# Attention and two feed-forward layers on one core: softmax sums from a column of ones, more engine choices, a new order

## The chip, the core and the metric

The kernel runs on one core of a Trainium2 chip. A core has TensorE (matmul), VectorE, ScalarE, GpSimd and a queue, SyncE, from which the DMAs are issued here. The metric is the device time of one execution in microseconds; the median of three runs of the kernel before is 1056.15 us (1055.23 to 1056.76).

## What is computed

```python
scores = (1/sqrt(D)) * q @ k.T + bias      # B=4, H=8, S=576, D=64; bias from a small MLP over positions
scores = scores - max(scores); attn = exp(scores)
attn = attn / (sum(attn) + 1e-09)
x = attn @ v                               # to 2304 tokens x 512
h = x @ w_in;  g = s * relu(h)**2 + b;  x = g @ w_out        # layer 1, 512 -> 2048 -> 512
h = x @ w_in2; g = h - tanh(h);         out = g @ w_out2     # layer 2, 512 -> 2048 -> 512
```

The weights come in 64-bit floats and are converted on the chip; matrices are split into an upper and a lower 16-bit part, and a product is three matmuls.

## The kernel before

The program is a list of tasks that a planner puts in order when the kernel is built. `Schedule.add` takes a task with the engines that may run it and the planner's cost on each, its predecessors, a priority (a due time) and the buffers that it takes or uses. `forward` then walks through a modelled time and picks, among the tasks that can start first, the one of lowest priority. Tables at the top of the file steer it: `COST` and `XFER` scale the costs of operations and transfers, `ENGINE` and `ONLY` narrow a task or a kind of task to certain engines, `SHIFT` moves the priority of each task (names such as `u13.hi`: unit group 13, step `hi`). The order on each engine's queue in the chip is fixed by this plan.

Attention has 144 units of 128 rows by 576 keys, in 36 groups of four (`unit_tasks`, `unit_rest`). One unit runs: score matmuls (`qk`, line 1041, two buffers `sp`); bias added and row maximum taken on VectorE (`ttr`, 1073); the maximum is shifted by a constant (`mx_add`, 1081, VectorE or GpSimd); the exponential on ScalarE (`ex`, 1087), which also accumulates the row sum into a column of `sum`; the upper 16-bit part (`hi`, 1097 on VectorE, 1099 on ScalarE); the lower part in two pieces (`lo_a`, `lo_b`, 1104, VectorE or GpSimd); a transposing DMA (`tr`, 1119); and the product with the values (`pv`, 1132 and 1138), nine and five matmuls of 64 columns into `xp`. There is one `xp` buffer for a group of four units. `x_tasks` then turns a group into tokens: epsilon on the sums (1176), reciprocal (1180), scaling of `xp` to `xf` (1188), which frees `xp`, upper and lower part, squares, and a transposing DMA.

`moe1_tasks` is layer 1, in nine blocks of 256 tokens: `ph` matmuls (1573), rectifier on ScalarE (1586), square (1591), upper and lower part (1597, 1599, 1603), `po` matmuls (1645), evacuation (1659, 1664). Layer 1 runs between the units of attention and goes on behind them. When attention has ended its buffers are given up (`turn`), and the weights of layer 2 are loaded, converted (1253, 1256, 1259), and split into seven combinations for each half (`w2_split`: upper part 615, sums 1852, lower part 618). Layer 2 (`in_product`, line 2038, and `out_product`, line 2166) is 18 half blocks of seven products each way. An `in_product` is evacuated to SBUF on ScalarE (`copy`, 2057) or VectorE (2064), goes through `tanh` (2074) and a subtraction (2083), and is combined with others (2092) and split for the next product. Before, `ONLY` keeps the subtractions, additions and sums of this part on VectorE.

Of the kernel before, what the change touches and what calls it, by code (L numbers as in the profile page):

```python
# [2326 lines left out]
```

## Time and profile before

| | |
|---|---|
| median of three runs | 1056.15 us |
| the profiled execution | 1057.96 us |
| its span, first to last instruction | 1056.2 us |
| TensorE matmul busy | 964.1 us (91%) |
| VectorE busy | 881.6 us (83%) |
| ScalarE busy | 667.5 us (63%) |
| GpSimd busy | 250.1 us (24%) |
| mean granted TensorE clock | 0.954 |

Busy shares are means over parts of the run with different limits. The rows further down give them by stretch, then who waits for whom, then the cost of single operations. In them PE is TensorE, PEld its weight load, DVE VectorE, ACT ScalarE, POOL GpSimd; a granted clock of 1.00 is the 2.4 GHz level, 0.50 the 1.2 GHz level.

### The profile page before, as it was taken

The page shows a single profiled execution, that of the slowest core. Times are in us where ns is not written, and L with a number is a line of the kernel's source. Part 1 is how long each engine was busy: PE and PEld are TensorE (multiplying, and loading weights), DVE is VectorE, ACT ScalarE, POOL GpSimd, SP SyncE. Part 2 cuts the span into 40 slices and gives each one's busy share as a digit, 9 for nine tenths or more (in the row PEclk, how much of TensorE's full clock was granted, in tenths as well). Part 3 has the DMA queues.
Part 4 walks back from the last instruction along what each step waited for, and adds up shares of the span by engine and source line. Part 5 has one row for each costly group of instructions (what it writes and reads, how often), then busy time and mean ns, then how long its engine had stood idle before and what let it go on. Part 6 is the DMA issues. An engine that isn't in the chain of part 4 may idle for free.

```text
span 1056.2 us, 32450 instructions
## 1 busy us (share of the span) xinstructions
PE 964.1 (91%) x13486; PEld 833.2 (79%) x13486; DVE 881.6 (83%) x1918; ACT 667.5 (63%) x1307; POOL 250.1 (24%) x319
## 2 busy tenths in 40 slices
PE   5676678999988999999997999988999999999998
PEld 3233356778767788788886888878999999999998
DVE  6999899876568677786774889999999999999885
ACT  4797659749767565776853687766554555464452
POOL 6146437247542334455511000000000000000000
PEclk9767679899999999999999999998999999999999
DMA  9969995899999879999896904410001100100000
GB/s 341 398 227 216 311 236 119 184 200 252 245 197 230 168 179 176 201 188 207 171 180 104 397 21 138 148 36 12 32 23 32 52 23 22 42 22 23 22 22 22
DMA packets 261444, 153.66 MB, mean 145 GB/s; under 512 B 197680, under 2 KB 229552, under 8 KB 261296
## 3 DMA queue, kind: packets, MB, share of 16 engines
q1 hardware_dynamic: 261296, 151.59, 59.1%
q8 instruction: 105, 1.72, 0.7%
q14 instruction: 43, 0.35, 0.1%
HBM read 84.03 MB, written 20.33 MB: 99 GB/s over the span
## 4 chain that ended last, share of the span: by engine, by line
PE 43%; DVE 9%; ACT 3%; DMA 2%; issue 2%; POOL 1%; SPq 0%; DVEq 0%; ACTq 0%; POOLq 0%
PE acc L2166 14%; PE pa L2038 9%; PE pb L2038 7%; PE po L1645 5%; PE ph L1573 4%; PE po L2166 2%; DMA et<-hl 2%; DVE w2big L1852 2%; DVE w2big L618 1%; PE sp L1041 1%; DVE w1big L618 1%; ACT e L1087 1%; POOL hl L1104 1%; PE xp L1132 1%; DVE hr L1603 1%
## 5 line engine op out<-in xcount | busy, mean ns | idle before, releaser
L1645 PE MATMUL po<-hr,w1big 128*128 128x256 f16 x1728 | 202.9, 274 | 3.6 <-ACT x L1664 2.7
L1104 POOL TENSOR_TENSOR hl<-e,hl 128x64 f16<-128x64 f32 (+1 forms) x200 | 160.2, 818 | 184.9 <-ACT hl L1099 107.2
L1573 PEld LDWEIGHTS <-w1big 128*128 128x128 f16 x1728 | 166.9, 99 | 31.5 <-issue 10.6
L1645 PEld LDWEIGHTS <-w1big 128*128 128x128 f16 x1728 | 165.5, 98 | 26.5 <-issue 7.1
L2038 PEld LDWEIGHTS <-w2big 128*128 128x128 f16 x3024 | 175.2, 99 | 2.2 <-issue 2.1
L2166 PEld LDWEIGHTS <-w1big 128*128 128x128 f16 x3024 | 172.8, 98 | 0.0
L1087 ACT ACTIVATE e<-sp,mx 128x576 f32<-128x576 f32 x144 | 105.6, 735 | 70.3 <-POOL mx L1081 34.3
L1073 DVE CUSTOM_DVE_ANT_0 sp<-sp,bi 128x576 f32<-128x576 f32 x144 | 107.0, 772 | 20.2 <-PE sp L1041 16.2
L1573 PE MATMUL ph<-xt_own,w1big 128*128 128x256 f16 x960 | 113.1, 274 | 3.0 <-ACT r L1586 2.2
L1041 PE MATMUL sp<-ks,qs 64*128 64x288 f16 (+1 forms) x960 | 84.2, 296 | 25.8 <-ACT e L1087 24.8
L1573 PE MATMUL ph<-w1big 128*128 128x256 f16 x768 | 91.2, 276 | 3.3 <-ACT r L1586 2.6
L1041 PEld LDWEIGHTS <-qs 64*128 64x128 f16 (+1 forms) x960 | 48.7, 99 | 53.0 <-issue 42.2
L1132 PEld LDWEIGHTS <-et 128*128 128x128 f16 (+1 forms) x1440 | 54.7, 104 | 41.2 <-issue 21.5
L1132 PE MATMUL xp<-vp,et 128*128 128x64 f16 (+1 forms) x1440 | 65.4, 199 | 19.1 <-DMA et<-hl 11.7
L2166 PE MATMUL acc<-hr,w1big 128*128 128x128 f16 x1296 | 79.9, 219 | 0.0
L1099 ACT ACTIVATE hl<-e 128x576 f16<-128x576 f32 x96 | 64.7, 678 | 23.1 <-DMA et<-hl 20.2
L2166 PE MATMUL acc<-w2big,w1big 128*128 128x128 f16 x1296 | 79.0, 219 | 0.0
L1104 DVE TENSOR_TENSOR hl<-e,hl 128x512 f16<-128x512 f32 (+1 forms) x88 | 48.8, 572 | 15.9 <-ACT hl L1099 13.0
L2038 PE MATMUL pa<-w1big,w2big 128*128 128x128 f16 x960 | 59.9, 219 | 1.7 <-ACT w2big L2057 0.9
L1586 ACT ACTIVATE r<-ph 128x512 f32<-128x512 f32 x72 | 42.3, 590 | 25.8 <-PE ph L1573 21.3
L1591 ACT ACTIVATE r<-r,sq 128x512 f32<-128x512 f32 x72 | 51.2, 718 | 0.9
L2074 ACT ACTIVATE w1big<-w1big 128x512 f32<-128x512 f32 x34 | 21.3, 630 | 45.6 <-DVE w1big L2064 33.4
(229 smaller groups left out, 1757.7 us busy)
## 6 DMA issues: line engine op xcount, KB each, us to landing
bi<-btd SPq DMA_DIRECT2D x64, 288.0 KB, 4.1
w1big<-in_wout SPq DMA_DIRECT2D x12, 1024.0 KB, 6.0
btd<-et SPq DMA_DIRECT2D x36, 295.5 KB, 3.7
w1big<-in_win SPq DMA_DIRECT2D x8, 1024.0 KB, 9.7
w2big<-in_win SPq DMA_DIRECT2D x8, 1024.0 KB, 13.1
x2d<-x SPq DMA_DIRECT2D x36, 128.0 KB, 3.1
w1big<-x2d SPq DMA_DIRECT2D x36, 128.0 KB, 2.3
outT<-xt_own SPq DMA_DIRECT2D x18, 256.0 KB, 2.2
```

The costliest lines, as they stand in the source:

```text
L1041: nc.tensor.matmul(out=out, lhsT=qs.tile[64 * h:64 * h + 64, sq, p * r:p * r + r], rhs=ks.tile[64 * h:64 * h + 64, sk, half * HS:(half + 1 ...
L1073: nc.vector.tensor_tensor_reduce(out=st, in0=st, in1=bi.tile.rearrange("p (a b) -> p a b", a=2), scale=-1.0 / KAP, scalar=3.0e38, op0=ALU. ...
L1087: nc.scalar.activation(out=put(e, row_tile("e")).rearrange("p (a b) -> p a b", a=2), in_=sp.tile[:, :, 0:HS], func=AF.Exp, scale=-1.0, bia ...
L1099: nc.scalar.activation(out=h[:, 0:S], in_=e.tile, func=AF.Copy)
L1104: eng_of(eng).tensor_tensor(out=hl.tile[:, o:o + m], in0=e.tile[:, c:c + m], in1=hl.tile[:, c:c + m], op=ALU.subtract)
L1132: nc.tensor.matmul(out=xp[r0:r0 + r, o:o + 64], lhsT=et.tile[:, n, r0:r0 + r], rhs=vp.tile[:, 0, n % 5, 64 * h:64 * h + 64], start=n == 0, ...
L1573: nc.tensor.matmul(out=ph.tile[:, fi, :], lhsT=win_ap(1, sw, m, f), rhs=xa(sx, m), start=m == 0 and j == 0, stop=m == KM - 1 and j == 2,)
L1586: nc.scalar.activation(out=r.tile, in_=ph.tile, func=AF.Relu)
L1591: nc.scalar.activation(out=r.tile, in_=r.tile, func=AF.Square, scale=sq[:, fp // 4:fp // 4 + 1])
L1645: nc.tensor.matmul(out=po.tile[:, :NB1], lhsT=wout_ap(1, sw, f, c), rhs=rhl[f // 8][:, f % 8, sr, :], start=f == 0 and j == 0, stop=f == K ...
L2038: nc.tensor.matmul(out=bank.tile[:, f * HT:(f + 1) * HT], lhsT=w[:, sw, m, f * 128:(f + 1) * 128], rhs=xs[:, sx, m], start=p in (1, 2, 5) ...
L2166: nc.tensor.matmul(out=bank.tile[:, o + c * HT:o + (c + 1) * HT], lhsT=w[:, sw, f, c * 128:(c + 1) * 128], rhs=g[:, sx, f], start=new and ...
```

## The change

The row sums no longer come from the exponential. The upper part of the values gets a 65th column of ones for each head, so that the product's 65th column is the row sum, and epsilon and reciprocal move behind the product. The shift of the maximum may run on ScalarE, the rectifier of layer 1 on VectorE; the upper halves of layer 2's weights on VectorE or GpSimd as well as ScalarE; the copies of layer 2 on VectorE too, the upper halves of its activations on GpSimd too. The sums of layer 2's weights lose GpSimd. `ONLY` is emptied, and `ENGINE` has 187 entries for 124, among them `"I5.lambda": "pool"`, `"I9.fn": "pool"` and the like for layer 2, and `f0.relu` to `f8.relu` but `f3.relu` on `act`. All entries of `SHIFT` are new, some constants of the planner move.

```diff
-    "u.ex@act": 0.848, "u.hi@act": 0.904, "bias.lambda@act": 1.1, "f.relu@act": 0.952, "f.square@act": 1.15,
+    "u.ex@act": 0.848, "u.hi@act": 1.1413, "bias.lambda@act": 1.1, "f.relu@act": 0.952, "f.square@act": 1.15,
...
-    "scan.fn": (0.80982, 2.01), "u.fn": (1.21869, 1.21), "u.tr": (1.0197, 2.23), "v.fn": (0.97218, 2.27),
+    "scan.fn": (0.80982, 1.99), "u.fn": (1.21869, 0.83), "u.tr": (1.0197, 2.23), "v.fn": (0.97218, 2.25),
...
+    "u12.lo_a": "pool", "u12.lo_b": "pool", "u13.lo_a": "pool", "u13.lo_b": "pool", "u17.lo_b": "pool",
+    "u7.lo_b": "dve", "f7.lo": "dve", "u4.lo_b": "dve", "u18.lo_b": "dve", "u5.hi": "dve", "u4.mx_add": "act",
+    "u7.hi": "act", "u17.lo_a": "pool", "f6.lo": "dve", "f8.hi": "dve", "u13.mx_add": "pool", "u1.lo_a": "pool",
+    "u6.mx_add": "pool", "f5.lo": "pool", "x18.hi": "act", "x13.lo": "pool", "bias2.lambda": "act", "v2.hi":
+    "act", "I5.lambda": "pool", "I0.lambda": "act+pool", "f2.lo": "dve", "u9.lo_b": "pool", "f5.hi": "act",
+    "u1.hi": "act", "u3.mx_add": "pool", "u1.lo_b": "pool", "x14.hi": "dve", "x0.lo": "dve", "x1.lo": "dve",
+    "u4.lo_a": "dve", "x17.lo": "pool", "I0.fn": "pool", "I0.sub": "dve", "I1.lambda": "dve", "I1.sub": "dve",
+    "I4.lambda": "act+dve", "I7.lambda": "act+pool", "X0.xsum": "dve", "bias1.lambda": "act+dve",
+    "bias3.lambda": "act+dve", "f0.relu": "act", "f1.relu": "act", "f2.relu": "act", "f4.relu": "act",
+    "f5.relu": "act", "f6.relu": "act", "f8.relu": "act", "u16.mx_add": "dve+pool", "u17.mx_add": "dve+pool",
+    "u18.mx_add": "act+pool", "s0.lambda": "dve+pool", "I9.lambda": "pool", "P10.lambda": "act+pool", "f1.out":
+    "dve", "u14.mx_add": "dve+pool", "bias4.out": "act", "u16.hi": "act", "u9.hi": "dve", "I9.fn": "pool",
+    "I11.add": "pool", "X2.xsum": "pool", "I17.lambda": "act+dve", "u18.lo_a": "pool", "I3.lambda": "act+pool",
+    "u14.lo_a": "pool", "I14.add": "pool", "I2.fn": "pool", "I15.lambda": "act+dve", "I11.fn": "dve", "I10.fn":
+    "dve", "u8.lo_a": "pool", "x6.lo": "pool", "s2.lambda": "dve+pool", "s6.lambda": "act+pool", "I12.add":
+    "dve", "J11.c22": "dve", "x7.lo": "dve", "x9.lo": "pool", "I8.sub": "pool", "k2.hi": "act", "I1.add":
+    "pool", "s4.lambda": "dve+pool", "I11.lambda": "act+dve", "f0.out": "dve", "f4.out": "dve", "I12.sub":
+    "dve", "u3.lo_a": "dve", "I2.lambda": "act", "X1.lambda": "dve", "I8.add": "dve", "s5.lambda": "act",
+    "bias1.out": "act", "I2.sub": "dve", "f6.hi": "act", "u7.lo_a": "dve", "I13.sub": "dve", "f7.relu": "act",
+    "P00.lambda": "act+pool", "x4.hi": "act", "I6.add": "pool", "X7.lambda": "act", "X1.xsum": "dve", "f8.out":
+    "act", "J5.c22": "dve", "x3.lo": "pool", "I16.lambda": "dve+pool", "f7.out": "act", "I0.add": "dve",
+    "x2.lo": "pool", "I7.add": "pool", "u8.hi": "act", "x5.hi": "act", "x7.hi": "act", "I14.fn": "pool",
+    "u9.lo_a": "dve", "u4.hi": "act", "I5.sub": "pool", "v0.ones": "dve", "f2.out": "act", "J9.fn": "pool",
+    "s7.lambda": "act+pool", "X4.lambda": "act", "I17.fn": "pool", "I10.sub": "dve", "I15.fn": "dve", "x1.hi":
+    "act", "X5.xsum": "dve", "u15.lo_a": "pool", "I13.fn": "pool", "X8.lambda": "act", "J13.fn": "pool",
+    "I16.sub": "pool", "I5.add": "dve", "I5.fn": "dve", "I13.add": "dve", "I10.add": "dve", "I17.add": "dve",
+    "P01.lambda": "act+dve", "J1.fn": "dve", "X6.lambda": "dve", "X5.lambda": "act", "J5.fn": "dve",
+    "I12.lambda": "pool", "I14.lambda": "act+pool", "I4.sub": "pool", "u2.hi": "act", "J3.fn": "dve", "J7.fn":
+    "pool", "x14.lo": "dve", "k3.hi": "dve", "J3.c22": "pool", "X7.xsum": "dve", "u5.mx_add": "act+pool",
+    "I9.add": "pool", "J13.c22": "pool", "I6.fn": "dve", "x17.hi": "dve", "X4.xsum": "dve", "x12.hi": "dve",
+    "x0.hi": "dve", "X3.lambda": "act", "u3.hi": "act", "I11.sub": "pool", "J15.c22": "pool", "I15.sub": "dve",
...
-ONLY = {"I.fn": "dve", "I.sub": "dve", "J.fn": "dve", "J.c22": "dve", "I.add": "dve", "X.xsum": "dve", "P.wsum": "dve"}
+ONLY = {}
...
-    xp_all = ps_x.tile([128, 256], F32, name="xp")
+    xp_all = ps_x.tile([128, 260], F32, name="xp")
...
+            t = vp_p.tile([128, 2 * VW + 10], F16, tag="vp", name="vp")
+            put(vp, (
+                t[:, :VW + 10].rearrange("p (n h d) -> p n h d", h=2, d=65),
+                t[:, VW + 10:].rearrange("p (n h d) -> p n h d", h=2, d=64),
+            ))
...
+        def ones(eng):
+            eng_of(eng).memset(vp.tile[0][:, :, :, 64:65], 1.0)
+        to = sc.add({POOL: 0.2, DVE: 0.1}, ones, [th], due - 2, [], [vp])
...
+            if eng == ACT:
+                nc.scalar.activation(out=m, in_=m, func=AF.Copy, bias=LN_E)
...
-        t_mx = sc.add({DVE: 0.16, POOL: 0.3}, mx_add, [t_ttr[u]], d + 1.5)
+        t_mx = sc.add({DVE: 0.16, POOL: 0.3, ACT: 0.2}, mx_add, [t_ttr[u]], d + 1.5)
...
-                scale=-1.0, bias=mx["m"][:, 0:1], accum_out=sm_i.tile[:, col:col + 1],
+                scale=-1.0, bias=mx["m"][:, 0:1],
...
-                        out=xp[r0:r0 + r, o:o + 64], lhsT=et.tile[:, n, r0:r0 + r],
-                        rhs=vp.tile[:, 0, n % 5, 64 * h:64 * h + 64], start=n == 0, stop=False,
+                        out=xp[r0:r0 + r, o:o + 65], lhsT=et.tile[:, n, r0:r0 + r],
+                        rhs=vp.tile[0][:, n % 5, h], start=n == 0, stop=False,
...
-        te = sc.add({DVE: 0.16, POOL: 0.3}, eps, [t_exp[u] for u in us], d - 3, [], [sum_of[n]])
+            nc.vector.tensor_scalar(
+                out=t, in0=x65()[:, :, 64], scalar1=1e-9 * 2.0 ** 15, scalar2=None, op0=ALU.add
+            )
+        te = sc.add({DVE: 0.18}, eps, [t_pv[u] for u in us], d - 502, [sums], [xp_of[n]], share=0.0)
...
-            tr = sc.add({ACT: 0.21 + 0.8e-3 * 2 * w}, relu, tp + [t_bs], ready - 400, [r], [ph])
+            tr = sc.add(
+                {ACT: 0.21 + 0.8e-3 * 2 * w, DVE: 0.12 + 1.05e-3 * 2 * w}, relu, tp + [t_bs], ready - 400, [r], [ph],
+                share=0.0,
+            )
...
-                {ACT: 1.14}, lambda e: copy_scale(dst(0), src(), w2s["c", g], e), deps + [t_w2c[g]], prio + o
+                {ACT: 1.14, DVE: 0.72, POOL: 3.0}, lambda e: copy_scale(dst(0), src(), w2s["c", g], e), deps + [t_w2c[g]], prio + o
...
-            return [sc.add({POOL: 2.5, DVE: 1.21}, wsum, deps, prio + o)]
+            return [sc.add({DVE: 1.21}, wsum, deps, prio + o)]
...
-                {ACT: 0.68}, lambda _: nc.scalar.activation(out=home(i), in_=bank.tile, func=AF.Copy, scale=ich),
-                [t] + (first_use["E"] if k < 2 else []), pr - 300, [i], [bank],
+                {ACT: 0.68, DVE: 0.66}, lambda e: copy_scale(home(i), bank.tile, ich, e),
+                [t] + (first_use["E"] if k < 2 else []), pr - 300, [i], [bank], share=0.0,
...
-                {ACT: 0.72, DVE: 0.49}, lambda e: copy_scale(dst(0), i.tile, names["cg"], e), [st["tG", n]] + war, o, [], [i]
+                {ACT: 0.72, DVE: 0.49, POOL: 1.6}, lambda e: copy_scale(dst(0), i.tile, names["cg"], e), [st["tG", n]] + war, o, [], [i]
```

## Rows read from the trace of the kernel before

**Rows 1.** Busy time by stretch: PE, PEld, DVE, ACT, POOL; then PEclk, DMA share, GB/s

```profile
0.00:200.00 200.00, 140.10 (x1507) 84.81 (x1508) 179.98 (x370) 148.20 (x301) 93.49 (x81) 0.80 0.90 259
200.00:560.00 360.00, 348.06 (x4641) 289.25 (x4637) 261.43 (x719) 246.24 (x557) 154.96 (x236) 1.00 0.99 198
560.00:740.00 180.00, 163.78 (x1768) 147.10 (x1767) 155.14 (x261) 119.90 (x223) 1.64 (x3) 0.97 0.38 120
740.00:1050.00 310.00, 310.00 (x5546) 310.00 (x5544) 283.05 (x565) 153.17 (x230) 0.00 (x0) 1.00 0.09 27
```

**Rows 2.** The chain that ended last, shares of the span by engine

```profile
PE 43%; DVE 9%; ACT 3%; DMA 2%; issue 2%; POOL 1%; SPq 0%; DVEq 0%; ACTq 0%; POOLq 0%
```

**Rows 3.** TensorE's waits, 60 to 200 us: total us, times, longest

```profile
PE sp L1041 <- ACT e L1087: 18.2, 20, 2.6
```

**Rows 4.** TensorE's waits, 200 to 560 us

```profile
PE sp L1041 <- ACT e L1087: 6.6, 10, 2.3
```

**Rows 5.** TensorE's waits, 560 to 730 us

```profile
PE psum L695 <- DVE w2big L2064: 3.9, 1, 3.9
PE pa L2038 <- ACT w2big L2057: 0.9, 1, 0.9
PE pa L2038 <- ACT w1big L2057: 0.8, 1, 0.8
```

**Rows 6.** Groups by line and shape: busy us, mean ns, idle before

```profile
L1087 ACT ACTIVATION_READ_ACCUMULATOR e<-sp,mx 128x1 f32 x144 | 28.1, 195 | 0.0
...
L1176 DVE TENSOR_SCALAR sum<-sum 128x4 f32<-128x4 f32 x29 | 5.5, 189 | 11.9 <-ACT e L1087 11.7
...
L1099 ACT ACTIVATE hl<-e 128x576 f16<-128x576 f32 x96 | 64.7, 678 | 23.1 <-DMA et<-hl 20.2 <-ACT e L1087 2.0 <-ACT r L1591 0.5
...
L1104 POOL TENSOR_TENSOR hl<-e,hl 128x512 f16<-128x512 f32 x86 | 103.2, 1202 | 49.6 <-ACT hl L1099 16.2 <-DVE hl L1097 13.1 <-issue 10.7
...
L2083 DVE TENSOR_TENSOR w1big<-w1big 128x512 f32<-128x512 f32 x34 | 23.3, 688 | 6.1 <-ACT w1big L2074 5.8
...
L613 POOL TENSOR_SCALAR w1big<-w1big,w1o_c 128x1024 f16<-128x1024 f32 x3 | 9.4, 3144 | 2.5 <-DVE w1big L618 1.7 <-DVE w1o_ic L488 0.8
```

**Rows 7.** The chain from 720 us: start, length, matmuls

```profile
721.13 5.28 PE pb L2038 x48
...
761.59 2.68 PE pb L2038 x48
```

**Rows 8.** Busy time of 721 to 726 us, columns as in rows 1

```profile
721.00:726.00 5.00, 4.90 (x48) 4.91 (x48) 5.00 (x10) 3.81 (x6) 0.00 (x0) 0.50 0.02 5
```

**Rows 9.** Timeline, 303 to 305 us: start, length, instruction

```profile
303.04 0.44 PE L1132 MATMUL xp<-vp,et 128*128 128x64 f16 x9 [1.13 <-DMA et<-hl]
...
303.31 0.31 PE L1138 MATMUL xp<-vp,et 128*128 128x64 f16 x5
...
304.03 0.72 ACT L1087 ACTIVATE e<-sp,mx 128x576 f32<-128x576 f32 x1
...
304.65 0.19 ACT L1087 ACTIVATION_READ_ACCUMULATOR e<-sp,mx 128x1 f32 x1
...
304.75 0.71 ACT L1591 ACTIVATE r<-r,sq 128x512 f32<-128x512 f32 x1
```

**Rows 10.** Timeline: scaling and next product, first and last of the twelve

```profile
89.82 0.41 DVE L1188 TENSOR_TENSOR xf<-xp,sum 128x256 f32<-128x256 f32 x1
...
90.28 0.42 PE L1132 MATMUL xp<-vp,et 128*128 128x64 f16 x9 [2.05 <-DVE xf L1188]
...
521.43 0.42 DVE L1188 TENSOR_TENSOR xf<-xp,sum 128x256 f32<-128x256 f32 x1
...
522.06 0.43 PE L1132 MATMUL xp<-vp,et 128*128 128x64 f16 x9
```

**Rows 11.** Instructions of lines 1259 and 1104: min/median/max ns

```profile
L1259 DVE SCALAR_TENSOR_TENSOR w1big<-w1big x16: 1194/1220/2227, 25.7 to 144.2; 128x1024 uint32<-128x1024 uint32 x16
...
L1104 DVE TENSOR_TENSOR hl<-e,hl x88: 192/684/1645, 64.8 to 564.3; 128x512 f16<-128x512 f32 x58, 128x64 f16<-128x64 f32 x30
```

More of the change, by code (lines that the diff above doesn't have):

```diff
@@ L86 @@
 EPS, WINDOW, IDLE, BUSY = 0.02, 3.4, 0.6, 0.9
 SHIFT = {
-    ".begin": 158.6, ".eye": 204.2, ".fn": -49.3, ".lambda": 60.6, "I0.add": 1197.4, "I0.fn": -551.5,
[120 rows of a table removed]
+    ".begin": -191.3, ".eye": 37.3, ".fn": 175.6, ".lambda": -216.5, "I0.add": 16.5, "I0.fn": -971.2,
[121 rows of a table added]
 }
@@ L286, in add @@
         only = ENGINE.get(t.key) or ONLY.get(kind)
+        if only is not None and not any(e in only for e in opts):
+            only = None
         t.opts = {}
@@ L290, in add @@
                 if isinstance(c, tuple):
-                    k, d = XFER.get(kind, (0.99, 1.79))
+                    k, d = XFER.get(kind, (0.99, 1.77))
                     t.opts[e] = (c[0] * 0.95 * COST.get(kind + "@" + e, 1.0), c[1] * k, d)
@@ L1025, in unit_tasks @@
         if k == 0:
-            sum_of[n], xp_of[n] = inst("sum"), inst("x")
-        sm_i, xp_i = sum_of[n], xp_of[n]
+            xp_of[n] = inst("x")
+        xp_i = xp_of[n]
         s_of[u] = sp
@@ L1172, in x_tasks, with eps @@
         us = list(range(4 * n, 4 * n + 4))
-        def eps(eng):
-            ri = sum_of[n].tile
-            eng_of(eng).tensor_scalar(out=ri, in0=ri, scalar1=1e-9 * 2.0 ** 15, scalar2=None, op0=ALU.add)
-        te = sc.add({DVE: 0.16, POOL: 0.3}, eps, [t_exp[u] for u in us], d - 3, [], [sum_of[n]])
+        sums = inst("sum")
+        x65 = lambda: xp_of[n].tile.rearrange("p (h d) -> p h d", d=65)
+        def eps(_):
+            t = put(sums, sm.tile([128, NP], F32, tag="sum", name="sum"))
+            nc.vector.tensor_scalar(
+                out=t, in0=x65()[:, :, 64], scalar1=1e-9 * 2.0 ** 15, scalar2=None, op0=ALU.add
+            )
+        te = sc.add({DVE: 0.18}, eps, [t_pv[u] for u in us], d - 502, [sums], [xp_of[n]], share=0.0)
         def recip(_):
-            nc.vector.reciprocal(out=sum_of[n].tile, in_=sum_of[n].tile)
-        te = sc.add({DVE: 0.17}, recip, [te], d - 2, [], [sum_of[n]])
+            nc.vector.reciprocal(out=sums.tile, in_=sums.tile)
+        te = sc.add({DVE: 0.17}, recip, [te], d - 501, [], [sums])
         xf = inst("xf")
         def scale(_):
-            x = xp_of[n].tile.rearrange("p (h d) -> p h d", d=64)
+            x = x65()[:, :, 0:64]
             put(xf, x_p.tile([128, 256], F32, tag="xf", name="xf", bufs=2))
@@ L1189, in scale @@
                 out=xf.tile.rearrange("p (h d) -> p h d", d=64), in0=x,
-                in1=sum_of[n].tile.unsqueeze(2).to_broadcast([128, NP, 64]), op=ALU.mult,
+                in1=sums.tile.unsqueeze(2).to_broadcast([128, NP, 64]), op=ALU.mult,
             )
-        t_xs[n] = sc.add({DVE: 0.41}, scale, [t_pv[u] for u in us] + [te], d - 500, [xf], [sum_of[n], xp_of[n]], share=0.0)
+        t_xs[n] = sc.add({DVE: 0.41}, scale, [te], d - 500, [xf], [sums, xp_of[n]], share=0.0)
         def hi(eng):
@@ L1414, in tile_kernel @@
     ]
-    v_done = lambda b: [x for p in range(NP) for x in (t_vhi[b, p], t_vlo[b, p])] + [x[1] for x in t_ssq[b]["v"]]
+    v_done = lambda b: [x for p in range(NP) for x in [t_vhi[b, p]] + t_vlo[b, p]] + [x[1] for x in t_ssq[b]["v"]]
     dest = [k_done(0, (0, 1)), k_done(0, (2, 3)), k_done(1, (0, 1)), k_done(1, (2, 3))]
```

60 lines of the change are left out of this document (28 added, 32 removed), and 255 rows, old and new, of tables (ENGINE, SHIFT).

## The prediction

> **What bounds the kernel now.** I read four views in this order. First the busy times by stretch [rows 1]: the span falls into four parts with different limits. From 0 to 200 us VectorE works 180.0 of 200 us and TensorE only 140.1, at 0.80 of its clock; VectorE is the limit. From 200 to 560 us TensorE works 348.1 of 360 at full clock: softmax units and layer 1 share it, and 11.9 us are idle. From 560 to 740 us TensorE works 163.8 of 180 beside a VectorE that is busy converting and splitting the weights of layer 2; 16.2 us are idle. From 740 to 1050 us TensorE has not one idle microsecond. Second, the chain that ended last [rows 2]: 43% of the span is TensorE's own matmuls, 9% VectorE and 3% ScalarE, so an engine other than TensorE matters only where TensorE is seen to wait for it. Third, these waits by stretch [rows 3 to 5]. Fourth, the groups by line, for the price of each operation [rows 6].
>
> Two conclusions steer the rest. Nothing done to layer 2 after 740 us can shorten the run, it can only lengthen it. And what can be won is the lost time ahead of that: 11.9 + 16.2 us of TensorE idle, a stretch at about the lower clock level behind the longest of these gaps, worth 2.6 us (the same 48 matmuls take 5.28 us at 721 and 2.68 us at 762, and the granted clock from 721 to 726 is 0.50 [rows 7, 8]), and 200 - 180.0 = 20.0 us in which VectorE, the limit of the first part, does nothing: about 51 us.
>
> **The change part by part.**
>
> *Row sums out of the exponential.* Each of the 144 exponentials is followed by an accumulator read of 195 ns [rows 6]. It is not all saved: in the timeline the exponential starts at 304.03, and the next ScalarE instruction at 304.75, although the exponential itself takes 0.72 and another engine step begins some 0.10 us before its forerunner's row ends; the read (304.65, 0.19) adds about 0.10 us to ScalarE's occupation [rows 9]. So ScalarE gains 144 x 0.10 = 14 us, but it is busy only 148 to 246 us in parts of 200 and 360 [rows 1] and is not the limit. What counts is where TensorE waits for an exponential before the next score matmul: 20 times in 60 to 200 us and 10 times after [rows 3, 4]. At 0.10 us each that is 3.0 us; the bounds are 30 x 0.195 = 5.9 us and nothing (where VectorE's reduction is as late). I take -3.0 us.
>
> *The 65th column.* 1440 matmuls of the value product grow from 64 to 65 columns. Nine of them take 303.31 - 303.04 = 0.27 us, 30 ns each [rows 9], so 1/64 more is 0.47 ns, and 1440 of them 0.7 us. No row has a moving operand of odd length. The far bound is the next wider row, 128 columns: 24 in 1.34 us, 56 ns (half of the 2.68 us for 48 [rows 7]); if an odd width cost as much, it would be 1440 x 26 ns = 37 us. 65 is nearest to 64, so I take +0.7 us and keep the other as a rival.
>
> *Epsilon and reciprocal behind the product.* Before, both run on the sums while the products are still going. Now they read the product's last column, so that they stand between the last product and the scaling that frees the only buffer `xp`. Each is a small VectorE step of 189 ns [rows 6], together 0.38 us. It costs where the next group's first product starts on the heels of the scaling. Following all 36 scalings in the timeline, that product begins within 0.45 us of the scaling's end in 12 cases, of which the first and the last are shown [rows 10]; elsewhere TensorE has other matmuls queued for longer. All 12 would be +4.6 us; a new order can put a block of layer 1 in between, then it is nothing. I take half, +2.3 us. Queued behind these steps on VectorE are the reductions of the next units; all 36 epsilons on VectorE instead of 29 are 1.3 us of it in 560, which I cost at nothing.
>
> *Ones, and the maximum's shift on ScalarE.* 16 memsets of one column hide in GpSimd's idle time (107 us of the first 200 [rows 1]) and come once for each head pair and batch; without that cover they would cost a few tenths of a microsecond each on VectorE. The shift of the row maximum may now go to ScalarE; the engine table does so for certain in group 4 alone, and groups 5 and 18 choose between ScalarE and GpSimd. It shortens a wait of ScalarE, which has slack. Zero.
>
> *More engines in the second half.* The table pins the new choice of VectorE for the layer-1 rectifier away again in eight of nine blocks (`f0` to `f8` but `f3`), so that part is nearly nothing. The upper halves of layer 2's weights may go to GpSimd, all but idle from 560 us on [rows 1]. In 704 to 714 us TensorE waits 0.9 and 0.8 us for evacuations on ScalarE that are queued behind such splits [rows 5]; taking splits off ScalarE gives up to -1.7 us, which I take; if VectorE takes them instead, it is nothing. The layer-2 subtractions and additions that move to GpSimd lie behind a full TensorE: no gain.
>
> *The order.* What remains is the order itself. Of the 51 us above some 5 are already counted. The largest pieces are of the kind that an order can mend: 3.9 us where TensorE waits behind VectorE's evacuation at 720 us with the low clock after it (2.6 us) [rows 5, 7], 6.6 us of score waits [rows 4]. The planner's cost of the exponentials' upper part (`u.hi`), 0.60 x 0.904 = 0.54 us on ScalarE, becomes 0.60 x 1.1413 = 0.685 us, and the row is 678 ns, 96 times [rows 6]: the new plan is nearer to the trace there. But no row says how much of the rest a new order finds; it can also lose. I take an eighth of 46 us, -6 us, between +5 and -25.
>
> The sum: -3.0 + 0.7 + 2.3 - 1.7 - 6 = -7.7 us. The profiled execution has 1057.96 us, of which 1056.2 are the span; it lies 1.8 us above the median of 1056.15, so 1050.3 for a like execution and 1048.5 against the median.
>
> **A rule against the change.** Where GpSimd works beside VectorE, single VectorE instructions are far above their usual time: the conversion step of line 1259 has 1220 ns in the middle and 2227 at most, the subtraction of line 1104 684 and 1645 [rows 11]; in layer 2, with GpSimd idle, the subtraction of line 2083 keeps a mean of 688 [rows 6]. The Trainium skill (SBUF — State Buffer, Who interferes with whom) says that VectorE and GpSimd share one port pair under an exclusive lock, and that a VectorE instruction with two SBUF inputs is blocked by a GpSimd instruction that reads SBUF for its whole length. The extra 1.0 us in these rows agrees with it; what it would do to layer 2 is the first of the rivals.
>
> **The rivals.**
>
> *Blocked VectorE in layer 2 (slower).* By the table at least 45 subtractions and additions (24 `fn`, 15 `sub`, 6 `add`) and 21 upper halves of layer 2 must run on GpSimd: 45 x 1.20 us and 21 x 1.57 us (an estimate: half of 3.14 us for twice the length [rows 6]), 87 us. VectorE loses 45 x 0.69 = 31 us of its 283 us in 740 to 1050 us, 252 are left [rows 1, 6]. The slack to 310 is 58 us. If more than 58 of the 87 us, two thirds, block VectorE, TensorE begins to wait; at five sixths it is 252 + 72 - 310 = +14 us, at all of it +29. For it: the rows above. Against it: the VectorE steps that read PSUM have one SBUF input only, and the planner keeps the two apart. With the other terms that gives 1062 us, and 1077 at all of it.
>
> *The longer release of `xp` (slower).* If in the 12 cases the two steps also queue behind another VectorE step of 0.69 us [rows 6], each costs 1.07 us, 12.8 us in all for 2.3 in the sum: 1059 us. Against it: before, the scaling waited in the same queue.
>
> *Odd width (slower).* 37 us, most of them where TensorE is full: 1075 to 1085 us. Nothing in the trace speaks for it but the absence of a row.
>
> *No change.* The new order finds nothing, and the small terms cancel (-1.7): 1054.5 us.
>
> *A better order.* Half of the 46 us: 1031 us. Against it: the old order already leaves TensorE 97% busy from 200 us on.
>
> **How the numbers follow.** Chances: forecast 0.52 (1038 to 1053.5), better order 0.11, no change 0.12, blocked VectorE 0.13, longer release 0.08, odd width 0.04. A measurement can tell about 0.2%, 2.1 us, from no change: faster 0.63, same 0.12, slower 0.25. For the range I leave out odd width, the upper half of the blocked case and the lower half of the better order, 0.16: 1034 to 1064 us.
>
> **What would show it.** Row sums: no accumulator reads behind the exponentials, fewer or shorter waits of score matmuls for them. Column: nine products in about 0.27 us still; 0.5 us would mean odd width. Release: waits of the product for the scaling, 5.2 us in 2 cases before, rise to some 8 us. Layer 2: GpSimd busy behind 740 us with TensorE still without gaps, and the wait at 720 us gone; line-2083 and line-2092 steps well above 0.69 us with TensorE waits would show blocking. The forecast is wrong if TensorE's idle time between 200 and 740 us is not below 28 us, or if layer 2 is no longer full.

## The result and the profile after

The changed kernel takes 1071.51 us (median) beside 1056.45 us of the kernel before on the same chip: ratio 1.0141, 95% interval 1.0124 to 1.0159, slower by 14.9 us. The forecast was 1048.5 us. To compare runs of different chips, the text below gives each as an excess over the kernel before in the same job: (ratio - 1) x 1056 us.

TensorE's busy total is 964.1 us, as before; what grew is its idle time. The busy times of the changed kernel by stretch, columns as in [rows 1]:

```profile
0.00:200.00 200.00, 138.71 (x1517) 86.06 (x1518) 181.91 (x367) 148.37 (x281) 93.97 (x78) 0.82 0.90 257
200.00:560.00 360.00, 347.29 (x4693) 287.48 (x4692) 251.12 (x682) 248.59 (x480) 179.68 (x261) 1.00 1.01 201
560.00:740.00 180.00, 156.91 (x1582) 140.06 (x1581) 156.41 (x251) 98.37 (x187) 46.95 (x15) 0.95 0.33 114
740.00:1050.00 310.00, 305.43 (x5423) 304.87 (x5421) 274.83 (x472) 126.66 (x190) 187.53 (x126) 0.99 0.09 28
```

Against [rows 1] TensorE loses 1.4, 0.8, 6.9 and 4.6 us, together the 13.6 us by which the span grew (1069.8 for 1056.2). Half of it goes where attention ends and layer 2 is prepared. ScalarE, busy 119.9 us there before, has 98.4 us; GpSimd, with 1.6 before, has 47.0. The second loss is behind 740 us, where TensorE was full.

TensorE's longest waits (total, times, longest): in the changed kernel in 60 to 200 and 200 to 560 us, then those for the transposing DMA in the kernel before in the same two stretches, then in the changed kernel in 560 to 760 us:

```profile
PE sp L1065 <- ACT e L1112: 15.4, 12, 4.5
PE xp L1156 <- DMA et<-hl: 9.6, 4, 4.6
...
PE xp L1156 <- DMA et<-hl: 5.4, 6, 1.7
...
PE sp L1065 <- ACT e L1112: 1.2, 2, 0.9
```

```profile
PE xp L1132 <- DMA et<-hl: 6.1, 5, 1.9
...
PE xp L1132 <- DMA et<-hl: 3.1, 5, 1.1
```

```profile
PE pb L2073 <- DVE w2big L2099: 4.7, 1, 4.7
PE psum L710 <- DVE cols L1931: 4.3, 1, 4.3
PE ph L1602 <- ACT r L1618: 3.3, 2, 2.1
PE po L1680 <- DVE hr L1638: 2.9, 2, 2.5
PE pa L2073 <- DVE w1big L626: 2.3, 1, 2.3
PE pb L2073 <- DVE cols L1934: 2.3, 1, 2.3
```

The score waits are shorter and fewer than in [rows 3, 4] (16.6 us, 14 times, for 24.8 us, 30 times), but the idle time of these stretches did not fall: waits for the transposing DMA rose from 9.2 to 15.0 us, and shorter ones came up. In the third stretch five of the six longest waits end with VectorE. VectorE itself waits there, for GpSimd. The timeline of GpSimd and VectorE in the changed kernel (start, length, instruction):

```profile
610.22 3.16 POOL L628 TENSOR_SCALAR w2big<-w2big,w_c 128x1024 f16<-128x1024 f32 x1 [51.58 <-ACT r L1626]
617.54 6.22 POOL L628 TENSOR_SCALAR w2big<-w2big,w_c 128x1024 f16<-128x1024 f32 x1 [4.17 <-DVE w2big L1887]
627.80 7.27 POOL L628 TENSOR_SCALAR w2big<-w2big,w_c 128x1024 f16<-128x1024 f32 x1 [4.04 <-DVE w2big L1887]
684.30 2.84 POOL L628 TENSOR_SCALAR w1big<-w2big,w_c 128x1024 f16<-128x1024 f32 x1 [49.23 <-DVE cols L1934]
...
631.76 0.68 DVE L1638 TENSOR_TENSOR hr<-r,hr 128x512 f16<-128x512 f32 x1
635.10 1.28 DVE L633 SCALAR_TENSOR_TENSOR w2big<-w2big,w_c 128x1024 f16<-128x1024 f32 x1 [2.67 <-POOL w2big L628]
```

These are upper halves of layer 2's weights, a step that took ScalarE 1.14 us before:

```profile
L615 ACT ACTIVATE w2big<-w2big,w_c 128x1024 f16<-128x1024 f32 x14 | 16.0, 1140 | 3.7 <-DVE w2big L1852 3.7
```

On GpSimd the same shape takes 2.84 us where it begins beside VectorE's small steps and 7.27 us where VectorE goes from one large step into the next; VectorE then has nothing left that may run (631.76 + 0.68 = 632.44) and stands 2.67 us until the split is there. A second stand of this kind, 2.66 us, comes at 700 us.

### The profile page after: what moved, and what is told of

It reads as the page before. It is cut to its first block, busy times and chain, and to the rows that moved or that the text cites. A ratio compares the mean times of both kernels' runs of the same rounds, so it can differ in the third digit from the quotient of the medians.

```text
span 1069.8 us, 32448 instructions
## 1 busy us (share of the span) xinstructions
PE 964.1 (90%) x13486; PEld 834.1 (78%) x13486; DVE 875.7 (82%) x1785; ACT 628.5 (59%) x1147; POOL 515.7 (48%) x484
## 4 chain that ended last, share of the span: by engine, by line
PE 42%; DVE 10%; DMA 5%; ACT 4%; POOL 3%; issue 3%; SPq 1%; DVEq 0%; ACTq 0%; POOLq 0%
PE acc L2201 12%; PE pa L2073 8%; PE po L1680 6%; PE pb L2073 6%; PE ph L1602 4%; DMA et<-hl 4%; PE po L2201 2%; DVE w1big L633 1%; DVE w2big L1887 1%; PE sp L1065 1%; ACT e L1112 1%; ACT hl L1123 1%; PE xp L1156 1%; POOL w2big L628 1%; POOL hr L628 1%
## 5 line engine op out<-in xcount | busy, mean ns | idle before, releaser
L1128 POOL TENSOR_TENSOR hl<-e,hl 128x64 f16<-128x64 f32 (+1 forms) x204 | 169.1, 845 | 140.8 <-ACT hl L1123 61.8
L2073 PEld LDWEIGHTS <-w2big 128*128 128x128 f16 x3024 | 178.1, 100 | 12.0 <-issue 11.8
L1065 PE MATMUL sp<-ks,qs 64*128 64x288 f16 (+1 forms) x960 | 81.9, 295 | 16.7 <-ACT e L1112 16.6
L1156 PE MATMUL xp<-vp,et 128*128 128x65 f16 (+1 forms) x1440 | 66.5, 198 | 17.7 <-DMA et<-hl 15.5
L1123 ACT ACTIVATE hl<-e 128x576 f16<-128x576 f32 x103 | 69.6, 680 | 21.9 <-DMA et<-hl 18.8
L2073 PE MATMUL pa<-w1big,w2big 128*128 128x128 f16 x960 | 62.4, 224 | 3.5 <-DVE w1big L626 2.3
L2073 PE MATMUL pb<-w1big,w2big 128*128 128x128 f16 x720 | 46.6, 226 | 7.8 <-DVE w2big L2099 4.7
```

Source lines behind the costliest of these rows:

```text
L1065: nc.tensor.matmul(out=out, lhsT=qs.tile[64 * h:64 * h + 64, sq, p * r:p * r + r], rhs=ks.tile[64 * h:64 * h + 64, sk, half * HS:(half + 1 ...
L1123: nc.scalar.activation(out=h[:, 0:S], in_=e.tile, func=AF.Copy)
L1128: eng_of(eng).tensor_tensor(out=hl.tile[:, o:o + m], in0=e.tile[:, c:c + m], in1=hl.tile[:, c:c + m], op=ALU.subtract)
L1156: nc.tensor.matmul(out=xp[r0:r0 + r, o:o + 65], lhsT=et.tile[:, n, r0:r0 + r], rhs=vp.tile[0][:, n % 5, h], start=n == 0, stop=False,)
L2073: nc.tensor.matmul(out=bank.tile[:, f * HT:(f + 1) * HT], lhsT=w[:, sw, m, f * 128:(f + 1) * 128], rhs=xs[:, sx, m], start=p in (1, 2, 5) ...
```

## The experiments

Line numbers of the experiments' kernels are shifted by the lines that an edit adds. All change only which engine a planned step is issued on, unless said otherwise: the plan is made as in the kernel named, and the engine replaced when the step is written out, so that the order of all steps stays. The excess over the kernel before, in us:

| run | excess (95% interval) |
|---|---|
| the changed kernel | 14.9 (13.1 to 16.8) |
| e1: its six weight splits off GpSimd | 6.9 (4.3 to 9.4) |
| e2: its other layer-2 steps off GpSimd | 11.8 (9.6 to 14.0) |
| e3: both | 5.5 (3.5 to 7.5) |
| e5: all layer-2 engines as before | 4.1 (1.8 to 6.4) |
| e11: as e5, no wait for the sums | 5.0 (2.9 to 7.2) |
| e12: half of each weight split off GpSimd | 12.8 (9.6 to 15.8) |
| e4: row sums alone, order of before | 0.7 (-1.3 to 2.7) |
| e7: as e4, no wait for the sums | -2.7 (-4.8 to -0.8) |
| e9: as e4, no epsilon | -0.4 (-3.0 to 2.1) |
| e6: before, layer-2 engines of the changed kernel | 64.4 (59.9 to 69.0) |
| e8: new attention, layer 2 of before, planned again | 5.8 (3.6 to 8.0) |
| e10: row sums, tables of before, planned again | 15.6 (12.9 to 18.4) |

**GpSimd's steps in layer 2: e1, e2, e3.** The edit of e3; e1 has the first two lines of the function only, e2 the other two:

```diff
+def remap(key, eng):
+    if eng == "pool" and key[0] == "P":
+        return "act"
+    if eng == "pool" and key[0] in "IJX":
+        return "act" if key.endswith(".lambda") else "dve"
+    return eng
...
-                t.fn(eng)
+                t.fn(remap(t.key, eng))
```

> The kernel after with its plan untouched; when the instructions are written out, the six upper halves of layer 2's weights that the plan gives to GpSimd (128x1024) go to ScalarE instead, at the same place in the order. Theory G (GpSimd's work around the start of layer 2 lies on the chain: two of these splits take 7.28 and 6.27 us there, against 1.14 on ScalarE): 1060 to 1067 us against 1071.5. Rival O (the searched order itself is worse, whichever engine runs a step): 1069 to 1074. Rival R (the row sums from the product cost the time): 1069 to 1074.

> The kernel after with its plan untouched; the steps of layer 2's blocks that the plan gives to GpSimd go elsewhere when they are written out: subtractions, additions and sums to VectorE, upper halves of activations to ScalarE. The weight splits stay on GpSimd. Theory G: 1061 to 1068 us, TensorE without gaps behind 760 us. Rival O: 1069 to 1074. The opposite, more load on VectorE where it is the limit: 1074 to 1080.

> Both edits of the two kernels above: nothing of layer 2 on GpSimd, plan untouched. Theory G: all of the loss is there, 1050 to 1060 us, since attention ends 7 us earlier than in the kernel before. Rivals O and R: not below 1068.

Measured: 1063.36, 1068.48 and 1060.42 us. e1 is inside theory G's interval, the other two a little above theirs; all three are below what the other theories allowed, e2 by 0.5 us only, which is within its error. Six splits are worth 14.9 - 6.9 = 8.0 us, the 139 other steps on GpSimd 3.1, both 9.4 us: close to two thirds of the loss. In e3 the stretch behind 740 us is full again, so the 4.6 us lost there belong to GpSimd's steps of both kinds (e1 and e2 alone leave 2.3 and 2.2 us):

```profile
560.00:740.00 180.00, 161.46 (x1681) 145.00 (x1680) 160.40 (x268) 108.71 (x201) 0.00 (x0) 0.96 0.34 116
740.00:1050.00 310.00, 310.00 (x5545) 310.00 (x5544) 279.27 (x552) 162.01 (x244) 0.00 (x0) 1.00 0.09 27
```

5.5 us over the kernel before are left.

How the splits reach TensorE is seen in e1's waits of 560 to 760 us. Of the six shown above, those for `cols` at line 1931 and for `hr` fall from 4.3 and 2.9 to 0.9 and 0.8 us; the longest, 4.7 us, stays as it is in e1, e2 and e3, so it is not owed to GpSimd:

```profile
PE psum L716 <- DVE cols L1937: 0.9, 1, 0.9
...
PE po L1686 <- DVE hr L1644: 0.8, 1, 0.8
```

The splits cost clock too. From 700 to 760 us, in the kernel before, the changed kernel and e1 (granted clock 0.94, 0.86 and 0.94; 0.86 in e2 too, which keeps the splits on GpSimd):

```profile
700.00:760.00 60.00, 54.34 (x878) 53.48 (x877) 57.33 (x105) 39.65 (x58) 0.00 (x0) 0.94 0.08 22
...
700.00:760.00 60.00, 44.45 (x650) 43.36 (x649) 55.90 (x81) 19.23 (x27) 29.38 (x15) 0.86 0.04 12
...
700.00:760.00 60.00, 46.49 (x765) 45.82 (x766) 56.50 (x94) 21.88 (x31) 29.94 (x16) 0.94 0.04 13
```

Of the 9.0 us by which e1's profiled execution is shorter than the changed kernel's, 4.2 are less idle time of TensorE and 4.8 less busy time (959.3 for 964.1 us), with the same matmuls. That the busy total of the changed kernel equals that of before is therefore a coincidence.

**What a split on GpSimd costs: e12.**

```diff
-                {ACT: 1.14, DVE: 0.72, POOL: 3.0}, lambda e: copy_scale(dst(0), src(), w2s["c", g], e), ...
+            def high(e):
+                if e == POOL:
+                    copy_scale(dst(0)[:, 0:512], src()[:, 0:512], w2s["c", g], POOL)
+                    copy_scale(dst(0)[:, 512:1024], src()[:, 512:1024], w2s["c", g], ACT)
```

> The changed kernel with each of its six weight splits on GpSimd cut in two: GpSimd takes columns 0 to 511, ScalarE columns 512 to 1023; order and everything else as in the changed kernel. In the changed kernel these six take 28.59 us of GpSimd (2.84 to 7.27 each, planned at 3.0), and taking them off GpSimd was worth 8.1 us (e1_splits_act). Theory D (the price is their length, VectorE's lower half waits for it, up to 2.7 us at a time): the halves take 1.4 to 3.7 us and about half of the 8.1 or more comes back, 1063 to 1068. Rival (the price is that they stand in GpSimd's queue and hand over to VectorE at all, whatever their length): 1069 to 1073, as the changed kernel.

Measured: 1068.84 us, just above theory D and just below the rival; by its ratio, 1.0121 (1.0091 to 1.0150), it cannot be told from the changed kernel. The time alone settles nothing, the rows do. GpSimd's timeline in e12, and VectorE's step behind its third split:

```profile
612.86 1.58 POOL L628 TENSOR_SCALAR w2big<-w2big,w_c 128x512 f16<-128x512 f32 x1 [51.65 <-ACT r L1626]
619.27 4.94 POOL L628 TENSOR_SCALAR w2big<-w2big,w_c 128x512 f16<-128x512 f32 x1 [4.83 <-DVE w2big L1892]
629.10 5.99 POOL L628 TENSOR_SCALAR w2big<-w2big,w_c 128x512 f16<-128x512 f32 x1 [4.89 <-DVE w2big L1892]
684.31 1.56 POOL L628 TENSOR_SCALAR w1big<-w2big,w_c 128x512 f16<-128x512 f32 x1 [49.22 <-DVE cols L1939]
...
635.12 1.28 DVE L633 SCALAR_TENSOR_TENSOR w2big<-w2big,w_c 128x1024 f16<-128x1024 f32 x1 [1.38 <-POOL w2big L628]
```

The shortest split shrank from 2.84 to 1.56 us, by 1.28. The two long ones shrank by the same 1.28, from 6.22 to 4.94 and from 7.27 to 5.99, and so did a third, further on (first the changed kernel, then e12):

```profile
693.99 6.26 POOL L628 TENSOR_SCALAR w1big<-w2big,w_c 128x1024 f16<-128x1024 f32 x1 [6.84 <-DVE w2big L1887]
...
694.00 4.98 POOL L628 TENSOR_SCALAR w1big<-w2big,w_c 128x512 f16<-128x512 f32 x1 [8.13 <-DVE w2big L1892]
```

What is left when a split's own time is taken off is equal in both kernels: 3.38 and 3.38 us, 4.43 and 4.43, 3.42 and 3.42. (The first split, which began among small steps and ran on beside copies, does not follow this: 3.16 and 1.58.) So a long row is read as a wait, which does not depend on the size, and then the work; VectorE's own stand fell by 1.29, from 2.67 to 1.38. The wait of the third split ends where VectorE's queue runs out: in e12, if its work is its last 1.56 us, it begins it at 633.53, while VectorE's last step before its stand lies at 633.06 to 633.74. That is not the only way in: the second split's wait ends, by the same reckoning, in the middle of VectorE's run (at 620.92 in the changed kernel), and VectorE's next lower half then takes longer than the 1.28 us shown above. What let GpSimd in there is not shown.

```profile
621.04 2.05 DVE L633 SCALAR_TENSOR_TENSOR w2big<-w2big,w_c 128x1024 f16<-128x1024 f32 x1
```

Theory D had the size of the price right for the part that is work, and missed that most of it is not.

**The other choices of engine: e5 and e6.** In e5 a table names for each of layer 2's 196 steps with another engine the one that the kernel before used, among them 32 copies and splits that the change had moved from ScalarE to VectorE. e6 is the mirror image.

```diff
-                t.fn(eng)
+                t.fn(MOVED.get(t.key, {}).get(nth[t], eng))
```

> The changed kernel's order of all steps is kept, and in layer 2 every step (weight splits, input splits, copies, differences, sums) is issued on the engine that the kernel before gave it: off GpSimd altogether, and 24 more upper halves and copies from VectorE back to ScalarE. Theory E (the choice of engines carries the whole loss; after both kinds of steps came off GpSimd 4.7 us were left, and in that run VectorE was busy 56.96 of the 60 us from 700 to 760 with about 10 splits and copies that ScalarE did before, ScalarE only 24.82): 1053 to 1057 us. Theory O (the new order at the start of layer 2, where the first products now come 8 us earlier than their inputs can be kept up, carries the rest): 1059 to 1062 us, no better than with both kinds off GpSimd.

> The mirror image: the kernel before, its order of all steps kept, row sums as before, and in layer 2 every step issued on the engine that the changed kernel gives it (6 weight splits, 51 activation splits, 83 differences and sums on GpSimd, some copies on VectorE). Theory E: 1066 to 1074 us, near the changed kernel's 1071.5. Theory O: 1057 to 1062 us. If the engines cost only in an order that was made for other durations, something between them.

Measured: 1059.98 and 1119.01 us. e5 is as slow as e3, so theory E falls for what e3 left: the steps moved between ScalarE and VectorE are worth nothing that can be measured. e6 fits neither theory. The same engines that cost some 10 us in the order that was planned for them cost 64 us in an order that was not. Its stretch behind 740 us, TensorE's waits from 770 us on, and the largest group of subtractions on GpSimd:

```profile
740.00:1050.00 310.00, 276.42 (x4700) 274.33 (x4698) 247.19 (x427) 116.94 (x177) 165.81 (x112) 0.96 0.08 24
```

```profile
PE psum L771 <- DVE cols L1972: 15.7, 6, 3.9
PE pa L2114 <- ACT w1big L2133: 8.4, 4, 4.1
PE pb L2114 <- ACT w2big L2133: 3.4, 4, 1.2
```

```profile
L2159 POOL TENSOR_TENSOR w1big<-w1big 128x512 f32<-128x512 f32 x15 | 20.3, 1355 | 35.1 <-ACT w1big L2150 35.1
```

No engine is full (VectorE 247.2 of 310 us, for 283.1 in [rows 1]), yet TensorE is idle for 33.6 us. A reading that fits, but that no run isolates: a step that takes 0.69 us on VectorE [rows 6] takes 1.36 us on GpSimd and comes later to a queue whose next step was due earlier, and everyone behind it waits in order. Not all of the 64 us is waiting: TensorE's busy total is 983.5 us for 964.1, with the same matmuls, and its granted clock in this stretch 0.96 for 1.00.

**The row sums: e4, e7, e9.** e4 keeps the plan of before; the exponential no longer accumulates, the values get the column of ones, and epsilon and reciprocal are issued directly ahead of the scaling:

```diff
-                scale=-1.0, bias=mx["m"][:, 0:1], accum_out=sm_i.tile[:, col:col + 1],
+                scale=-1.0, bias=mx["m"][:, 0:1],
...
-                        rhs=vp.tile[:, 0, n % 5, 64 * h:64 * h + 64], start=n == 0, stop=False,
+                        rhs=vp.tile[0][:, n % 5, h], start=n == 0, stop=False,
...
+            nc.vector.tensor_scalar(out=ri, in0=x65[:, :, 64], scalar1=1e-9 * 2.0 ** 15, scalar2=None, op0=ALU.add)
+            nc.vector.reciprocal(out=ri, in_=ri)
```

e7 puts a constant and its reciprocal where before had epsilon and reciprocal, and takes the two lines out (first part of the diff), so that its output is not normalised; e9 replaces them by one that reads the product's column (second part):

```diff
+            eng_of(eng).memset(sum_of[n].tile, 2.0 ** 24)
...
+            nc.vector.reciprocal(out=sum_of[n].tile, in_=sum_of[n].tile)
...
-            nc.vector.tensor_scalar(out=ri, in0=x65[:, :, 64], scalar1=1e-9 * 2.0 ** 15, scalar2=None, op0=ALU.add)
-            nc.vector.reciprocal(out=ri, in_=ri)
+            nc.vector.reciprocal(out=sum_of[n].tile, in_=x65[:, :, 64])
```

> The kernel before with its plan untouched and the row sums alone changed: no accumulator in the exponential, the column of ones, epsilon and reciprocal directly ahead of the scaling on VectorE. By the steps of the prediction -3.0 + 0.7 + 2.3 = 0: 1053 to 1060 us. Rival R: 1062 or more. The opposite, the accumulator read was on the chain all along: 1045 to 1052.

> Row sums alone on the order of before (as in the run e4_sums_alone), with the wait left out: the scaling divides by nothing that the product made, since a constant and its reciprocal are put where before had the epsilon and the reciprocal, so the output is not normalised. What is left of the change is the sums off ScalarE and the 65th column. By the prediction's terms (sums -3.0, 65th column +0.7, epsilon and reciprocal behind the product +2.3) this should be 2.3 us faster than e4's 1057.25, near 1055 and below the kernel before by about 1 to 2 us. If the two steps behind the product are free and the sums gained nothing, 1056 to 1058 like e4.

> Row sums alone on the order of before (e4_sums_alone), with one of the two steps behind the product taken out: the reciprocal reads the column of sums straight from the product's bank, and the epsilon is left out (1e-9 beside a sum of at least 1 changes no float32 value). Theory W (what the row sums gain on ScalarE, 2.6 us by e7 against before, is given back by the two steps on VectorE that each product's scaling waits for, 4.1 us by e7 against e4): about half of the 4.1 comes back, 1054.5 to 1056, at or 1 us below the kernel before. Rival (the price is the wait for the product at all, not the steps): 1057 as e4.

Measured: 1057.25, 1053.13 and 1054.48 us. e7 is faster than the kernel before, its whole interval below 1 (0.9955 to 0.9992); e4 is not. So row sums out of the exponential gain 2.7 us, and the two steps behind the product take 3.4 back, each within some 2 to 3 us. e9 lies between them, as theory W has it, but its interval holds e4 and e7 as well; it does not beat the kernel before. e7's score waits, in 60 to 200 and 200 to 560 us, are 21.9 us for 24.8:

```profile
PE sp L1048 <- ACT e L1094: 14.9, 18, 2.4
...
PE sp L1048 <- ACT e L1094: 7.0, 11, 1.6
```

One thing e7 does not separate: VectorE no longer stands 11.7 us for the exponentials ahead of epsilon [rows 6], since a constant needs none of them. Groups of e4 (the two steps; busy, mean ns, idle before):

```profile
L1197 DVE RECIPROCAL sum<-sum 128x4 f32<-128x4 f32 x36 | 6.4, 178 | 1.3
...
L1194 DVE TENSOR_SCALAR sum<-xp 128x4 f32<-128x4 f32 x36 | 5.6, 156 | 1.0 <-PE xp L1145 0.9
```

**The order: e8, e10, e11.** e8 takes the changed kernel's tables for attention and layer 1 and the tables and allowed engines of before for layer 2. e10 takes those of before throughout and adds the row-sum change to the plan. Neither uses GpSimd in layer 2, and both are planned anew. Their common edit of the changed kernel (the tables, too long to show, as said):

```diff
-                {ACT: 1.14, DVE: 0.72, POOL: 3.0}, lambda e: copy_scale(dst(0), src(), w2s["c", g], e), ...
+                {ACT: 1.14}, lambda e: copy_scale(dst(0), src(), w2s["c", g], e), ...
...
-                {ACT: 0.68, DVE: 0.66}, lambda e: copy_scale(home(i), bank.tile, ich, e),
+                {ACT: 0.68}, lambda e: copy_scale(home(i), bank.tile, ich, e),
...
-                {ACT: 0.72, DVE: 0.49, POOL: 1.6}, lambda e: copy_scale(dst(0), i.tile, names["cg"], e), ...
+                {ACT: 0.72, DVE: 0.49}, lambda e: copy_scale(dst(0), i.tile, names["cg"], e), ...
```

e11 is e5 with this edit:

```diff
-            nc.vector.tensor_scalar(
-                out=t, in0=x65()[:, :, 64], scalar1=1e-9 * 2.0 ** 15, scalar2=None, op0=ALU.add
-            )
+            nc.vector.memset(t, 2.0 ** 24)
```

> The changed kernel's tables for attention and layer 1 and its row sums, with the tables and the allowed engines of before for layer 2 (its weights, inputs, products), planned again. Theory E: at or below the kernel before, 1048 to 1058, since nothing runs on GpSimd in layer 2. Theory O says that any fresh plan of the start of layer 2 is a draw: anywhere from 1052 to 1068, with its loss between 560 and 760 us.

> The row-sum change alone with the tables and allowed engines of before throughout, planned again with the new steps in the plan, so that the whole order of the kernel changes and nothing else does. Theory O (the order of before is a found one, and any fresh one loses a few us, most of it between 560 and 760 us): 1059 to 1070. Rival (the planner, told of the new steps, places them where they don't delay anybody): 1052 to 1057.

> The changed kernel's order with the engines of before in layer 2 (e5_engines_of_before, 1059.98), and the epsilon replaced by a constant, so that neither it nor the reciprocal waits for the product; the output is not normalised. If the remaining 4.4 us over before are the two steps behind the product as in e4 (worth 4.1 there): 1055.5 to 1057. If they are the new order at 560 to 760 us: 1059 to 1061 as e5.

Measured: 1060.73, 1069.8 and 1059.44 us. All three are what theory O allowed. e10 is the sharpest: the same allowed engines, operations and tables as e4, but another order, and the excess is 15.6 us for 0.7. The planner also chose a few engines anew (8 of the 144 upper parts `hi` went from ScalarE to VectorE), which no run separates from the order. Its first, third and fourth stretch:

```profile
0.00:200.00 200.00, 142.86 (x1480) 82.63 (x1480) 179.64 (x373) 147.12 (x271) 93.85 (x85) 0.81 0.94 263
...
560.00:740.00 180.00, 160.61 (x1739) 142.59 (x1736) 154.63 (x266) 114.58 (x212) 2.43 (x4) 0.96 0.38 124
740.00:1050.00 310.00, 307.32 (x5490) 307.06 (x5489) 280.20 (x559) 152.04 (x231) 0.00 (x0) 1.00 0.09 26
```

The expectation put most of such a loss between 560 and 760 us. That was wrong: TensorE's idle time grows by 3.2 us there and by 2.7 behind it, and shrinks ahead of it; the span's other 7 us are longer busy time, whose cause stays open. e11, whose output is not normalised either, is no faster than e5, so in the new order the wait for the sums costs nothing that can be measured and cannot be the 4 to 5 us that e5 leaves. Where these lie stays open: e5's profiled execution, 1058.15 us, is 1.8 below its median, its span of 1056.4 us is that of before, and TensorE's extra idle time in it is spread over all stretches.

## Why the prediction was wrong, point by point

**What bounds the kernel.** The reading by stretch held: TensorE, full behind 740 us, could only lose there, and did, 4.6 us. The sum went from -7.7 to +14.9, 22.6 us, and two terms carry nearly all of that: the engines of the second half (-1.7 forecast, +9.4 measured) and the order (-6 forecast, +3.4 measured). The estimate that some 46 us lay open to a better order has no run behind it: none of the three new orders (the changed kernel's own, also with the old engines in e5; e8; e10) is faster than that of before.

**Row sums and the 65th column.** Forecast -3.0 + 0.7 = -2.3 us; e7 shows -2.7, and its score waits fell by 2.9. Right within the error, and the odd width is no rival: 1152 matmuls of the product in the changed kernel have the mean of before, 198 ns, and nine of them still take 302.92 - 302.65 = 0.27 us:

```profile
L1156 PE MATMUL xp<-vp,et 128*128 128x65 f16 x1152 | 59.0, 198 | 17.1 <-DMA et<-hl 14.9 <-DVE xf L1217 1.2 <-ACT vp L630 0.6
...
302.65 0.44 PE L1156 MATMUL xp<-vp,et 128*128 128x65 f16 x9
302.92 0.32 PE L1162 MATMUL xp<-vp,et 128*128 128x64 f16 x5
```

The ones cost less than the few tenths of a microsecond each that the prediction named for VectorE: six of the 16 memsets ran there, at 67 ns.

**Epsilon and reciprocal.** Forecast +2.3 between 0 and 4.6; 3.4 in the order of before (e4 against e7), nothing measurable in the new one (e11 against e5). The count behind the forecast was off: in the trace of before the next product begins within 0.45 us of the scaling's end in 9 cases, and in 12 only within 0.52. The forecast rise of the waits for the scaling to some 8 us did not come: they are 1.2 us, in the row just shown. The bounds held. The reason for the lower one, that a new order puts other work in between, fits this but was not tested by itself.

**More engines in the second half.** This step failed. It read "taking splits off ScalarE gives up to -1.7 us, which I take; if VectorE takes them instead, it is nothing", and so bounded the price by nothing, although the row of 3144 ns for the same shape on GpSimd stood in [rows 6], and a lower half on VectorE waits for each upper half. With sign and size it is +9.4 us; taking off those six splits alone brings 8.0 of it. The rule against the change was used for the wrong engine: it priced how long VectorE would be kept by GpSimd's many small steps behind 740 us. That happens. The lower halves there take 946 ns, for 746 before (first line):

```profile
L618 DVE SCALAR_TENSOR_TENSOR w2big<-w2big,cols 128x512 f16<-128x512 f32 x36 | 26.6, 746 | 0.7 <-ACT w2big L615 0.5
...
L633 DVE SCALAR_TENSOR_TENSOR w2big<-w2big,cols 128x512 f16<-128x512 f32 x34 | 31.8, 946 | 2.0 <-ACT w2big L630 1.9
```

But there the order leaves room for it: all these steps cost 3.1 us (e2), where the rival had 14 or 29, although GpSimd worked 187.5 us there and not the rival's 87. What costs is the reverse, GpSimd kept waiting by a VectorE that is busy 156 of 180 us, on a path where a weight split is due. The Trainium skill (SBUF — State Buffer, Who interferes with whom) says that the first to issue holds the shared ports for a whole instruction and that the other is then fully blocked; the equal waits of 3.38 and 4.43 us at full and half size agree with a block rather than a slowdown. They are longer than any one VectorE instruction that ran during them (1.27 us), so by these rows a blocked GpSimd can stand behind several of them. The other direction does not agree. A lower half that began 0.06 us behind a split took 2.13 us for 1.28, and ended at 702.41 us while the split ran to 703.06; in e12, beside a split of half the size, it took 1.70:

```profile
700.22 2.84 POOL L628 TENSOR_SCALAR w1big<-w2big,w_c 128x1024 f16<-128x1024 f32 x1
700.28 2.13 DVE L633 SCALAR_TENSOR_TENSOR w1big<-w2big,w_c,w1big 128x1024 f16<-128x1024 f32 x1 [2.66 <-POOL w1big L628]
...
699.01 1.70 DVE L633 SCALAR_TENSOR_TENSOR w1big<-w2big,w_c,w1big 128x1024 f16<-128x1024 f32 x1 [1.38 <-POOL w1big L628]
```

VectorE lost 0.85 and 0.42 us there, not the whole length of the split.

The statement that the differences and sums "lie behind a full TensorE: no gain" was right as far as it went; it should have been asked what they lose.

**The order.** Forecast -6 us, between +5 and -25. This term failed as well: for the changed kernel's own order, with its choices of engine in attention and layer 1, e5 less e4 gives 4.1 - 0.7 = +3.4 us, inside the bounds but on the other side of zero. The forecast took a share of the idle time as a gain although, as it said itself, no row told how much a new order finds; where the order loses instead stays open. For a fresh order in general the upper bound was too small: e10, planned from the old tables, has 15.6 - 0.7 = +14.9. The argument "the new plan is nearer to the trace there" (the cost of `u.hi`) was a reason for the attention part, where the score waits did shrink; the next wait, for the transposing DMA, took their place.

**The sum as it should have been:** row sums -2.7, the wait for them +3.4 in the old order, the order +3.4 (it takes the wait's 3.4 away, so that e11 less e7 makes the order by itself 7.7), the choice between VectorE and ScalarE +1.4 (e3 less e5, within the error), GpSimd in layer 2 +9.4: 14.9 us. The parts come from pairs of runs and each carries an error of some 2 to 3 us.

**The rivals.** The side came out as "Blocked VectorE in layer 2" had it, at 1071.5 us for 1062 to 1077, but at another place, with other steps and the roles of the two engines swapped, so that the agreement in time is luck. Of the tests named, idle time of TensorE between 200 and 740 us below 28 us failed (12.7 + 23.1 = 35.8), and so did a full layer 2; longer steps beside GpSimd with waits of TensorE were seen.

## What to carry to other kernels

A step that moves to an idle engine is priced by its length there and by who waits for its end, not by the room that it leaves behind; where the two engines hinder each other, its length on a busy stretch is a wait that the other engine sets plus its own work, and making it smaller shortens only the work. Gaps that open in TensorE's work can also cost it clock, so the loss is counted in idle and in busy time. An order that a search has found is part of the kernel: before crediting a new one with a share of the idle time, make the same edit once in the old order and once planned anew, and take the difference between these two as the size of the unknown. When an instruction moves behind a result that others wait for, the gain where it left and the wait where it goes are of one size here, within their errors (2.7 and 3.4 us), and one of them alone is half an estimate.

## What was not expected of the hardware

A GpSimd split that starts while VectorE works from one large instruction into the next makes no progress that the rows show: 3.38, 4.43 and 3.42 us pass, to 0.01 us the same for 1024 and 512 columns, and what is left is the 2.84 or 1.56 us that it takes beside small steps. In the other direction VectorE loses less than the split's length: the lower half above 0.85 of 2.84 us, and a step on 128x4 elements, 0.17 us otherwise, took 1.03 us as a split began (0.60 in e12):

```profile
610.12 0.17 DVE L495 TENSOR_SCALAR p2b<-p2a 128x4 uint32<-128x4 uint32 x1
610.33 1.03 DVE L499 TENSOR_SCALAR p2a<-p2b 128x4 uint32<-128x4 uint32 x1
```

A moving operand of 65 columns costs TensorE no more than one of 64 (198 ns in the mean for both).
